# Scale columns first: the first four heads without the shift, key groups on demand, and two moved side tasks

## The chip, the cores and the metric

One core of a Trainium2 chip runs the whole program. The metric is device time in microseconds (us), from repeated executions. The profiler's span is 1.7 to 1.9 us shorter than the device time of the same execution. On one core a slower state is only recognised by its distance from the fastest run. All kernels below gave correct results.

Names: PE is TensorE's matmul, PEld its weight load, DVE VectorE, ACT ScalarE, POOL GpSimd, SPq the queue that issues DMA. The kernel divides PSUM, which holds the results of matmuls, into eight banks, 0 to 7. "Granted clock" is the share of full speed that TensorE's clock was allowed.

## The reference, cut to what matters

```python
mod = (_silu(c) @ w_mod).reshape(c.shape[0], 6, 1, -1)
sa, ca, ga, sb, cb, gb = (mod[:, 0], mod[:, 1], mod[:, 2], mod[:, 3], mod[:, 4], mod[:, 5])
h = layernorm(x) * (1 + ca) + sa                 # x: 2048 x 1024
x = x + ga * attention(h, k_cache, v_cache, wq, wo)   # 32 heads of 128, 4 key groups, last 512 keys
h = layernorm(x) * (1 + cb) + sb
x = x + gb * ((silu(h @ w_gate) * (h @ w_up)) @ w_down)
```

The scale `ca` and the shift `sa` are needed before the first query projection. The rows are handled in four chunks of 512. The query of a head is `(n * (1 + ca) + sa) @ wq = (n * (1 + ca)) @ wq + sa @ wq`, where `n` is the normalised row; the second term is the same for all rows, so it is one column per head in the transposed layout that the kernel uses. The change rests on this identity.

## The kernel before

A helper waits for what each operation reads and writes; banks are such objects too. A bank can be written again only after its reader has finished. The program emits one list of instructions for each engine, in the order of the code below.

The prologue normalises the first chunk, computes scale and shift as 128 matmuls with a single column each (from eight 512 KB pieces of `w_mod`), and fills TensorE in between with `warm` products on zeros. `x_mod` writes the modulated input, four heads are projected, all 16 key tiles are transposed:

```python
def mod_mm(w_ap, wbuf, k, cols):
    for n, (j, o) in enumerate(cols):
        mm(bank(XB, 1, 2 * o), w_ap[:, j * P:(j + 1) * P], sc_bf[:, k:k + 1], ...)   # XB = 7: one column
...
for k in range(4, DT):
    warm(3, WB)
    mod_k(k)                       # 16 single-column products
warm(5, WB)
x_mod()                            # hT = psum * gain + shift, on DVE and ACT
for sl in range(2):
    for kc in range(sl * HK, (sl + 1) * HK):
        for h in range(LEAD + 1):  # four heads
            mm(bank(QB0[h]), wq_s[0][:, kc, h * P:(h + 1) * P], hT[0][:, kc, :], ...)
for idx in range(GK):              # 16 key transposes into banks 1 and 2
    transpose(bank_bf(SCB + 1 + idx // 8)[...], k_nat[:, idx, :], ...)
```

The main loop has one step per head. It projects head `i+3`, computes scores of head `i-1` and the PV product of head `i-2`, then runs one step of a background list `bg`. `row_task` broadcasts a row over all partitions: POOL makes diagonal matrices, TensorE multiplies them into bank XB, DVE copies the bank:

```python
def row_task(dst, dbuf, src, sbuf):
    T.op(POOL, lambda: g.tensor_copy(c6[:, :], src), ...)
    diags(0)                                        # four POOL products, 128x128
    yield
    for n in range(2):
        for q in range(4):
            mm(bank(XB, P, q * P), ones_bf, diag[q], ...)
        T.op(DVE, lambda: V.tensor_copy(dst[:, n * 512:(n + 1) * 512], bank(XB)), writes=[PB[XB], dbuf])
        if n == 0:
            diags(1)
        yield
...
LOADT = {Hq + 2 + (5 * n) // 2: n for n in range(NL)}   # loads of the later gate columns
bg.append(rows)                    # first row task: runs in heads 1 to 3
for i in range(1, NA + 2):
    if i == 8:
        add_ln1(1)                 # layernorm of the next chunk joins the background list
    if i + LEAD < NA:
        if (i + LEAD) % Hq == 0:
            finish(ln1[(i + LEAD) // Hq])
        qproj(i + LEAD)            # bank QB, evicted by DVE
    if i - 5 in LOADT:             # gate column used five heads after its load
        mod_col(n); ...            # the last one appends the row task of the last gate
    scores(i - 1); pv(i - 2)
    if h2 == Hq - 1 and ch2 < NCH - 1:
        finish(rows)               # a row task still open is forced here
        oproj(ch2)
    run_bg(1)
```

The softmax here doesn't subtract the row's maximum and nothing guards it: scores larger than these inputs give would overflow.

## Time and profile before

| | before |
|---|---|
| median of three runs | 1282.97 us (1281.84 to 1283.47) |
| span of the profiled run | 1280.5 us |
| PE busy | 1271.3 us (99%) |
| first projection can start (scale copied) | 19.77 us |
| first exponential | 31.86 us |
| first reciprocal (first PV product finished) | 35.60 us |
| one head in the steady state | 3.50 us |

The page of the kernel before, its part on the engines and its chain of waits (the chain that ended last, by engine):

```profile
PE 1271.3 (99%) x7632; PEld 645.9 (50%) x7632; DVE 474.9 (37%) x873; ACT 339.7 (27%) x382; POOL 42.1 (3%) x102
PE 99%; DVE 0%; DMA 0%; POOL 0%; issue 0%; ACT 0%; SPq 0%; POOLq 0%
```

TensorE is the limit, so only what TensorE waits for, or does needlessly, can be won. The list of PE's waits in the kernel before (who waited for whom, us in total, times, longest):

```profile
PE ps L369 <- DMA c_row<-in_c_dram: 3.6, 1, 3.6
PE ps L266 <- DVE rowb L567: 1.5, 1, 1.5
PE ps L266 <- DVE arena L394: 0.5, 1, 0.5
PE ps L266 <- POOL arena L559: 0.3, 1, 0.3
PE ps L266 <- DVE arena L455: 0.3, 1, 0.3
PE ps L266 <- ACT arena L633: 0.2, 1, 0.2
```

The `rowb` and `L559` lines are one stall near 482 us, the `L394` line is one near 129 us. The first, in the timeline of the kernel before (start, duration, engine, line, operation; idle time before it and what ended it in brackets):

```profile
481.93 2.35 POOL L559 TENSOR_SCALAR arena<-arena,c 128x128 bf16<-128x128 bf16 x4 [0.66 <-PE ps L266]
482.56 0.68 DVE L567 CAST rowb<-ps 128x512 bf16<-128x512 f32 x1
483.39 0.59 PE L266 MATMUL ps<-arena 128*128 128x128 bf16 x3 [1.47 <-DVE rowb L567]
484.33 8.00 PE L266 MATMUL ps<-arena 128*128 128x128 bf16 x37 [0.35 <-POOL arena L559]
```

The row task of the last gate is forced at the end of the third chunk. TensorE can go on only when POOL has made the last diagonal, at 484.33 us. The second stall is seen in the reciprocals, which follow one another once a head:

```profile
125.51 0.18 DVE L651 RECIPROCAL rl<-ps 128x4 f32<-128x4 f32 x1 [1.08 <-PE ps L266]
129.01 0.18 DVE L651 RECIPROCAL rl<-ps 128x4 f32<-128x4 f32 x1 [1.08 <-PE ps L266]
133.46 0.18 DVE L651 RECIPROCAL rl<-ps 128x4 f32<-128x4 f32 x1 [1.08 <-PE ps L266]
```

The normal distance is 3.50 us; from 129.01 to 133.46 it is 4.45 us. The next chunk's modulated input had to be finished there. The same view where the first row task runs, early in the loop:

```profile
35.60 0.18 DVE L651 RECIPROCAL rl<-ps 128x4 f32<-128x4 f32 x1 [1.46 <-PE ps L266]
35.82 0.69 DVE L654 TENSOR_TENSOR arena<-ps,rl 128x512 bf16<-128x512 f32 x1
36.43 0.68 DVE L567 CAST arena<-ps 128x512 bf16<-128x512 f32 x1
39.32 0.18 DVE L651 RECIPROCAL rl<-ps 128x4 f32<-128x4 f32 x1 [1.08 <-PE ps L266]
```

The copy of bank XB (L567) ends 1.51 us after the reciprocal has begun. Here nobody waits for it: the next reciprocal comes 3.72 us later, and the extra 0.22 us are the row task's own four products.

### The profile page before, as it was taken

To read this page: it belongs to the slowest core of one execution; us is meant where nothing else is said; L and a number is where in the kernel's file an instruction comes from. 1 tells how busy PE (TensorE), PEld (TensorE's weight loads), DVE (VectorE), ACT (ScalarE), POOL (GpSimd) and SP (SyncE) were. 2 spreads that over 40 slices of the span, in tenths; PEclk is the share of its full clock that TensorE was granted. 3 is DMA by queue.
4 is the path that set the end of the run, shared out by engine and by line. 5 is a ranking of instruction groups with operands and counts; after the bars stand their busy time and mean duration, and the time that the engine had idled before them with its cause. 6 is when DMAs were issued, how large, how long until landed. Compare 5 with 4: busy or idle time off the path is not lost.

```text
span 1280.5 us, 17793 instructions
## 1 busy us (share of the span) xinstructions
PE 1271.3 (99%) x7632; PEld 645.9 (50%) x7632; DVE 474.9 (37%) x873; ACT 339.7 (27%) x382; POOL 42.1 (3%) x102
## 2 busy tenths in 40 slices
PE   8999999999999999999999999999999999999999
PEld 4565545555455554455554444444444444444444
DVE  3455324664247652265422331233222331221222
ACT  3555303555025550055520111011100111011100
POOL 2010000000000001000000000000000000000000
PEclk9999999999999999999999999999999999999999
DMA  8999403866018641065352974046421754035200
GB/s 287 264 238 238 101 1 71 194 141 157 1 24 191 145 120 41 1 128 112 73 150 70 283 239 132 17 144 169 132 74 39 199 149 132 17 114 165 67 9 25
DMA packets 233742, 155.31 MB, mean 121 GB/s; under 512 B 128960, under 2 KB 219968, under 8 KB 233664
## 3 DMA queue, kind: packets, MB, share of 16 engines
q1 hardware_dynamic: 175424, 95.45, 31.0%
q10 hardware_dynamic: 58240, 58.72, 14.4%
q8 instruction: 60, 0.98, 0.3%
q14 instruction: 18, 0.15, 0.0%
HBM read 119.54 MB, written 4.19 MB: 97 GB/s over the span
## 4 chain that ended last, share of the span: by engine, by line
PE 99%; DVE 0%; DMA 0%; POOL 0%; issue 0%; ACT 0%; SPq 0%; POOLq 0%
PE ps L266 99%; PE ps L270 0%; DMA c_row<-in_c_dram 0%; POOL arena L559 0%; ACT arena L633 0%; DVE arena L654 0%; DVE arena L455 0%; DVE tmp L673 0%; DVE arena L675 0%; SPq L302 0%; DVE arena L394 0%; DVE rl L651 0%; DVE mod_bf L449 0%; PE ps L369 0%; DVE gain L435 0%
## 5 line engine op out<-in xcount | busy, mean ns | idle before, releaser
L266 PE MATMUL ps<-arena 128*128 128x512 bf16 (+2 forms) x7391 | 1266.5, 334 | 2.9 <-DVE rowb L567 1.5
L266 PEld LDWEIGHTS ps<-arena 128*128 128x128 bf16 x7391 | 636.6, 98 | 622.9 <-issue 3.0
L633 ACT ACTIVATE arena<-ps 128x1024 bf16<-128x1024 f32 x256 | 262.0, 1024 | 355.2 <-PE ps L266 343.5
L848 ACT ACTIVATE arena<-ps 128x512 bf16<-128x512 f32 x112 | 66.9, 597 | 506.1 <-PE ps L266 506.1
L849 DVE TENSOR_TENSOR arena<-ps,arena 128x512 bf16<-128x512 f32 x112 | 77.4, 692 | 276.2 <-PE ps L266 276.2
L673 DVE TENSOR_TENSOR tmp<-ps,rowb 128x512 f32<-128x512 f32 (+1 forms) x65 | 44.4, 683 | 319.3 <-PE ps L266 319.3
L590 DVE CAST arena<-ps 128x512 bf16<-128x512 f32 x124 | 85.6, 691 | 60.0 <-PE ps L266 60.0
L654 DVE TENSOR_TENSOR arena<-ps,rl 128x512 bf16<-128x512 f32 x128 | 88.5, 691 | 4.7 <-DVE rl L651 0.3
L651 DVE RECIPROCAL rl<-ps 128x4 f32<-128x4 f32 x128 | 23.3, 182 | 120.4 <-PE ps L266 120.4
L378 DVE BATCH_NORM_STATS2 st<-x_res 128x6 f32<-128x512 bf16 x62 | 42.3, 683 | 3.6 <-DMA x_res<-in_A_x_dram 3.5
L383 POOL TENSOR_SCALAR rstd<-mv 128x1 f32<-128x1 f32 x31 | 6.9, 224 | 887.8 <-DVE mv L382 887.8
L544 DVE SCALAR_TENSOR_TENSOR arena<-arena 128x1024 bf16<-128x1024 bf16 x24 | 29.2, 1215 | 0.0
L675 DVE TENSOR_TENSOR arena<-tmp,x_res 128x512 bf16<-128x512 f32 (+1 forms) x33 | 22.3, 676 | 1.1
L675 DVE TENSOR_TENSOR x_res<-tmp,x_res 128x512 bf16<-128x512 f32 x32 | 22.1, 692 | 1.1
L394 DVE TENSOR_SCALAR arena<-arena,gain,mod_bf 128x512 bf16<-128x512 bf16 x56 | 20.3, 405 | 0.0
L385 POOL TENSOR_TENSOR rstd<-rstd,mhalf 128x1 f32<-128x1 f32 x31 | 17.7, 570 | 2.6
L389 DVE TENSOR_SCALAR nsc<-x_res,mv,rstd 128x1024 bf16<-128x1024 bf16 x30 | 16.1, 538 | 0.9 <-POOL rstd L385 0.9
L559 POOL TENSOR_SCALAR arena<-arena,c 128x128 bf16<-128x128 bf16 x24 | 14.5, 620 | 23.9 <-PE ps L266 23.6
L266 PEld LDWEIGHTS ps<-sc_bf,arena 128*128 128x128 bf16 x192 | 7.1, 96 | 3.8
L266 PE MATMUL ps<-sc_bf,arena 128*128 128x1 bf16 x192 | 7.1, 163 | 0.0
L382 DVE BATCH_NORM_AGGREGATE mv<-st 128x2 f32<-128x12 f32 x31 | 6.5, 208 | 1.1
L459 ACT ACTIVATE arena<-ps,mod_bf,gain_f 128x512 bf16<-128x512 bf16 x3 | 2.2, 774 | 11.1 <-DVE arena L455 11.1
(44 smaller groups left out, 33.0 us busy)
## 6 DMA issues: line engine op xcount, KB each, us to landing
arena<-in_A_wq_dram SPq DMA_DIRECT2D x31, 1024.0 KB, 5.6
arena<-in_B_w_gate_dram ACTq DMA_DIRECT2D x28, 1024.0 KB, 5.3
arena<-in_B_w_up_dram ACTq DMA_DIRECT2D x28, 1024.0 KB, 7.9
arena<-in_A_wo_dram SPq DMA_DIRECT2D x8, 1024.0 KB, 6.1
arena<-in_B_w_down_dram SPq DMA_DIRECT2D x7, 1024.0 KB, 9.3
arena<-in_w_mod_dram SPq DMA_DIRECT2D x8, 512.0 KB, 8.2
out_dram<-arena SPq DMA_DIRECT2D x15, 256.0 KB, 2.0
x_res<-in_A_x_dram SPq DMA_DIRECT2D x3, 1024.0 KB, 6.4
```

The source lines that it names most:

```text
L266: T.op(PE, lambda: TE.matmul(out_ap, lhsT, rhs, start=start, stop=stop, skip_group_check=skip), reads=reads, writes=[bank_buf])
L378: T.op(DVE, lambda: V.bn_stats(st_[sl][:, hf * 6:hf * 6 + 6], x_res[:, t, hf * 512:hf * 512 + 512]), reads=[B_x[t]], writes=[B_st[sl]])
L394: T.op(DVE, lambda: V.tensor_scalar(dst[:, dt, :], dst[:, dt, :], gain[gi][:, dt:dt + 1], mod_bf[:, ccol + dt:ccol + dt + 1], op0=ALU.mult ...
L544: T.op(DVE, lambda: V.scalar_tensor_tensor(mt[n % 2], mt[n % 2], 1.0, sc_row, op0=ALU.mult, op1=ALU.mult, accum_out=mcol[:, n:n + 1]), rea ...
L590: T.op(DVE, lambda: V.tensor_copy(qT_s[qs], bank(QB)), writes=[PB[QB], B_qT[qs]])
L633: T.op(ACT, lambda: A.activation(ex_s[es][:, 2 * kp:2 * kp + 2, :], banks2(SCB + 2 * kp), AF.Exp, scale=att_scale), writes=[PB[SCB + 2 * k ...
L651: T.op(DVE, lambda: V.reciprocal(rl[r][:, :].rearrange("p (a b) -> p a b", a=2), psap(PVB * 512 + P, [[512, 2], [130, 2]])), writes=both + ...
L654: T.op(DVE, lambda: V.tensor_tensor(o_s[os_].rearrange("p (a b) d -> p a b d", a=2), psap(PVB * 512, [[512, 2], [130, 2], [1, P]]), rlb, A ...
L673: T.op(DVE, lambda: V.tensor_tensor(tmp[s][:, 0:n], bank(b, n), rowb[ri][:, c0:c0 + n], ALU.mult), reads=[B_row[ri]], writes=[PB[b], B_tmp ...
L675: T.op(DVE, lambda: V.tensor_tensor(dst[:, c0:c0 + n], tmp[s][:, 0:n], x_res[:, t, c0:c0 + n], ALU.add), reads=[B_tmp[s], B_x[t]], writes= ...
L848: T.op(ACT, lambda: A.activation(sg_s[ss], bank(gb), AF.Silu), writes=[PB[gb], B_sg[ss]])
L849: T.op(DVE, lambda: V.tensor_tensor(guT[:, ft, :], bank(ub), sg_s[ss], ALU.mult), reads=[B_sg[ss]], writes=[PB[ub], B_gu[ft]])
```

## The change

The intent: have the first projection wait for the scale columns only (2 MB of `w_mod` instead of 4 MB), bring the shift in later as one bias column per head for the first four heads, add it to the input for all others, transpose the key groups when they are needed, and start two background tasks earlier. The diff, cut to its core:

```diff
-            wme = [... eight pieces of scale and shift columns, 512 KB each ...]
+            wca = [... eight pieces of scale columns, 256 KB each, loaded first ...]
+            wsa = [... shift columns, loaded behind the first weights of the projection ...]
@@ prologue
-                mod_k(k)                    # 16 products, with warm(2) or warm(3)
+                mod_ca(k)                   # 8 products, with warm(2) or warm(1)
-                        ... V.tensor_scalar(hT[0][:, dt, :], src, gain, mod_bf, op0=ALU.mult, op1=ALU.add)
+                        ... V.tensor_scalar(hT[0][:, dt, :], src, gain, None, op0=ALU.mult)
@@ behind the projection of the first four heads
-            for idx in range(GK): transpose(...)            # all 16 key tiles
+            for k in range(DT):
+                mod_mm(wsa[:, k, :], B_wsa[k], k, MCOLS)    # 64 single-column products: the shift
+            T.op(DVE, ... mod_bf[:, 0:DT] <- bank XB)
+            k_turn(0, SCB + 1)                              # 4 key tiles
+            for h in range(LEAD + 1):                       # 32 single-column products: the bias
+                for kc in range(DT):
+                    mm(bank(SCB + 2, 1, 2 * h), wq_s[0][:, kc, h * P:(h + 1) * P], mod_bf[:, kc:kc + 1], ...)
+            for dt in range(DT):                            # hT += shift, in place
+                if dt < 4: DVE   elif dt < 6: ACT   else: POOL
+            ... the four evictions add bq[:, h:h + 1] (DVE and ACT)
@@ main loop
-            LOADT = {Hq + 2 + (5 * n) // 2: n for n in range(NL)}
+            LOADT = {Hq + 2 + (9 * n) // 4: n for n in range(NL)}
+                if 2 <= i < 1 + Hkv:
+                    k_turn(i - 1, XB)                       # key groups 1 to 3 through bank XB
+                    T.op(DVE, lambda: V.tensor_copy(kd, ks), writes=[PB[XB], B_kT[i - 1]])
-                if i == 8:
+                if i == 5:
                     add_ln1(1)
-                    qproj(i + LEAD)
+                    qproj(i + LEAD, SCB + 3 if i == 1 else QB)
-                if i - 5 in LOADT:
+                if i - 4 in LOADT:
```

The change also merges two reciprocal square roots on POOL into one and reorders some loads.

More of the change, by code (lines that the diff above doesn't have):

```diff
@@ L193, in bass_adaLN_cond__sliding_block_cached__swiglu_ffn__prompt_kernel @@
     mv = [S_("mv%d" % i, [P, 2], F32) for i in range(4)]
-    rstd = [S_("rstd%d" % i, [P, 1], F32) for i in range(4)]
+    rstd4 = S_("rstd4", [P, 4], F32)
+    rstd = [rstd4[:, i:i + 1] for i in range(4)]
+    bq = S_("bq", [P, 4], F32)
     rl = [S_("rl%d" % i, [P, 4], F32) for i in range(2)]
@@ L232, in bass_adaLN_cond__sliding_block_cached__swiglu_ffn__prompt_kernel @@
     B_cT = _Buf("cT"); B_sc = _Buf("sc"); B_late = [_Buf("late%d" % i) for i in range(4)]; B_c6 = _Buf("c6"); B_mcol = _Buf("mcol"); B_scr = _Buf("scr")
-    B_mode = _Buf("mode"); B_gf = _Buf("gf")
+    B_mode = _Buf("mode"); B_modc = _Buf("modc"); B_bq = _Buf("bq"); B_gf = _Buf("gf")
     B_nm = _Buf("nmean"); B_acc = _Buf("acc")
@@ L321, in _ @@
             HK = DT // 2
-            B_wme = [_Buf("wme%d" % k) for k in range(DT)]
-            wme = [arena.at(OFF_OT + k * 4 * KB, [NE * P], BF16, [B_wme[k]]) for k in range(DT)]
+            B_wca = [_Buf("wca%d" % k) for k in range(DT)]
+            B_wsa = [_Buf("wsa%d" % k) for k in range(DT)]
+            wca = [arena.at(OFF_OT + k * 2 * KB, [D], BF16, [B_wca[k]]) for k in range(DT)]
+            wsa = arena.at(OFF_OT + 16 * KB, [DT, D], BF16, B_wsa)
             for k in range(DT):
-                T.op(dq("q_wm%d" % k), lambda: SP.dma_start(wme[k], w_mod[k * P:(k + 1) * P, 0:NE * P]), writes=[B_wme[k]])
+                T.op(dq("q_wca%d" % k), lambda: SP.dma_start(wca[k], w_mod[k * P:(k + 1) * P, D:2 * D]), writes=[B_wca[k]])
             NWQ = 2
@@ L347, in _ @@
             load_wq0(1)
+            for k2 in range(DT // 2):
+                T.op(dq("q_wsa%d" % k2), lambda: SP.dma_start(
+                    wsa[:, 2 * k2:2 * k2 + 2, :],
+                    w_mod[2 * k2 * P:(2 * k2 + 2) * P, 0:D].rearrange("(k p) n -> p k n", p=P)), writes=B_wsa[2 * k2:2 * k2 + 2])
             B_kn = [_Buf("kn%d" % i) for i in range(Hkv)]
-            B_kT = _Buf("kT"); B_kT2 = _Buf("kT2"); B_va = _Buf("va")
-            k_nat = arena.at(OFF_KN, [GK, P], BF16, B_kn)
-            kT_sb = arena.at(OFF_KT, [GK, P], BF16, [B_kT, B_kT2])
+            B_kT = [_Buf("kT%d" % i) for i in range(Hkv)]
+            B_va = _Buf("va")
+            kT_sb = arena.at(OFF_KT, [GK, P], BF16, B_kT)
             VW = 160
@@ L356, in _, with load_k @@
             B_vg = [_Buf("vg%d" % i) for i in range(Hkv)]
-            for gk in range(Hkv):
+            hT = [arena.at(OFF_HT + i * 8 * KB, [DT, CH], BF16, []) for i in range(2)]
+            B_hT = [[_Buf("hT%d_%d" % (i, dt)) for dt in range(DT)] for i in range(2)]
+            for i in range(2):
+                arena.regs.append((OFF_HT + i * 8 * KB, OFF_HT + (i + 1) * 8 * KB, B_hT[i]))
+            k_nat = hT[1].rearrange("p a b -> p (a b)")[:, 0:GK * P].rearrange("p (a b) -> p a b", a=GK)
+            def load_k(gk):
                 T.op(Q_k[gk], lambda: SP.dma_start(k_nat[:, gk * KT:(gk + 1) * KT, :],
@@ L360, in _, with load_v @@
                      writes=[B_kn[gk]])
-            load_wq(1)
-            for gk in range(Hkv):
+            def load_v(gk):
                 T.op(Q_v[gk], lambda: SP.dma_start(v_aug[:, gk * KT:(gk + 1) * KT, 0:P],
@@ L365, in _ @@
                      writes=[B_vg[gk]])
+            load_k(0)
+            load_wq(1)
+            load_v(0)
+            load_x(1)
+            for gk in range(1, Hkv):
+                load_k(gk)
+            for gk in range(1, Hkv):
+                load_v(gk)
             T.op(POOL, lambda: g.memset(v_aug[:, :, P:P + 2], 1.0), writes=[B_va])
@@ L382, in aggr @@
                 T.op(DVE, lambda: V.bn_aggr(mv[sl][:, :], st_[sl][:, :]), reads=[B_st[sl]], writes=[B_mv[sl]])
-                T.op(POOL, lambda: g.tensor_scalar(rstd[sl][:, :], mv[sl][:, 1:2], eps, None, op0=ALU.add),
+                T.op(POOL, lambda: g.tensor_scalar(rstd[sl], mv[sl][:, 1:2], eps, None, op0=ALU.add),
                      reads=[B_mv[sl]], writes=[B_rs[sl]])
-                T.op(POOL, lambda: g.tensor_tensor(rstd[sl][:, :], rstd[sl][:, :], mhalf[:, 0:1], ALU.pow),
+                T.op(POOL, lambda: g.tensor_tensor(rstd[sl], rstd[sl], mhalf[:, 0:1], ALU.pow),
                      reads=[B_rs[sl], B_mh], writes=[B_rs[sl]])
             def norm(t, sl, ns):
-                T.op(DVE, lambda: V.tensor_scalar(nsc4[ns], x_res[:, t, :], mv[sl][:, 0:1], rstd[sl][:, 0:1],
+                T.op(DVE, lambda: V.tensor_scalar(nsc4[ns], x_res[:, t, :], mv[sl][:, 0:1], rstd[sl],
                                                   op0=ALU.subtract, op1=ALU.mult),
@@ L416, in ln_task @@
                         yield
-            hT = [arena.at(OFF_HT + i * 8 * KB, [DT, CH], BF16, []) for i in range(2)]
-            B_hT = [[_Buf("hT%d_%d" % (i, dt)) for dt in range(DT)] for i in range(2)]
-            for i in range(2):
-                arena.regs.append((OFF_HT + i * 8 * KB, OFF_HT + (i + 1) * 8 * KB, B_hT[i]))
             def mod_mm(w_ap, wbuf, k, cols):
@@ L448, in x_mod @@
             def x_mod():
-                T.op(DVE, lambda: V.tensor_copy(mod_bf[:, 0:NE], psap(XB * 512, [[2, NE]])), writes=[PB[XB], B_mode])
-                mod_gain(0, 0, DT, B_mode, B_g[0])
+                T.op(DVE, lambda: V.tensor_copy(mod_bf[:, DT:NE], psap(XB * 512, [[2, DT]])), writes=[PB[XB], B_modc])
+                mod_gain(0, 0, DT, B_modc, B_g[0])
                 T.op(DVE, lambda: V.tensor_copy(gain_f[:, :], gain[0][:, :]), reads=[B_g[0]], writes=[B_gf])
@@ L454, in x_mod, with mod_ca @@
                     if dt % 2 == 0 or dt == 5:
-                        T.op(DVE, lambda: V.tensor_scalar(hT[0][:, dt, :], src, gain[0][:, dt:dt + 1], mod_bf[:, dt:dt + 1],
-                                                          op0=ALU.mult, op1=ALU.add),
-                             reads=[B_g[0], B_mode], writes=[PB[dt // 2], B_hT[0][dt]])
-                    else:
-                        T.op(ACT, lambda: A.activation(hT[0][:, dt, :], src, AF.Identity,
-                                                       bias=mod_bf[:, dt:dt + 1], scale=gain_f[:, dt:dt + 1]),
-                             reads=[B_gf, B_mode], writes=[PB[dt // 2], B_hT[0][dt]])
-            ECOLS = [(j, j) for j in range(NE)]
-            def mod_k(k):
-                mod_mm(wme[k], B_wme[k], k, ECOLS)
+                        T.op(DVE, lambda: V.tensor_scalar(hT[0][:, dt, :], src, gain[0][:, dt:dt + 1], None, op0=ALU.mult),
+                             reads=[B_g[0]], writes=[PB[dt // 2], B_hT[0][dt]])
+                    else:
+                        T.op(ACT, lambda: A.activation(hT[0][:, dt, :], src, AF.Copy, scale=gain_f[:, dt:dt + 1]),
+                             reads=[B_gf], writes=[PB[dt // 2], B_hT[0][dt]])
+            MCOLS = [(j, j) for j in range(DT)]
+            def mod_ca(k):
+                mod_mm(wca[k], B_wca[k], k, MCOLS)
             tl = TPC - 1
-            def rstd_pow(t):
-                T.op(POOL, lambda: g.tensor_tensor(rstd[t][:, :], rstd[t][:, :], mhalf[:, 0:1], ALU.pow),
-                     reads=[B_rs[t], B_mh], writes=[B_rs[t]])
             T.op(ACT, lambda: A.activation(nsc4[tl], x_res[:, tl, :], AF.Copy, accum_out=acc[:, 0:1]),
@@ L496, in _ @@
             for k in range(3):
-                mod_k(k)
+                mod_ca(k)
                 warm(2, WB)
             stats(2, 2, 1)
-            aggr(2)
-            T.op(POOL, lambda: g.tensor_scalar(rstd[tl][:, :], acc[:, 1:2], 1.0 / D, eps, op0=ALU.mult, op1=ALU.add),
+            T.op(DVE, lambda: V.bn_aggr(mv[2][:, :], st_[2][:, :]), reads=[B_st[2]], writes=[B_mv[2]])
+            T.op(POOL, lambda: g.tensor_scalar(rstd[2], mv[2][:, 1:2], eps, None, op0=ALU.add),
+                 reads=[B_mv[2]], writes=[B_rs[2]])
+            T.op(POOL, lambda: g.tensor_scalar(rstd[tl], acc[:, 1:2], 1.0 / D, eps, op0=ALU.mult, op1=ALU.add),
                  reads=[B_acc], writes=[B_rs[tl]])
-            rstd_pow(tl)
+            T.op(POOL, lambda: g.tensor_tensor(rstd4[:, 2:4], rstd4[:, 2:4], mhalf[:, 0:2], ALU.pow),
+                 reads=[B_mh], writes=[B_rs[2], B_rs[tl]])
             norm(2, 2, 2)
             x_first(2)
-            warm(3, WB)
-            T.op(DVE, lambda: V.tensor_scalar(nsc4[tl], x_res[:, tl, :], nmean[:, 0:1], rstd[tl][:, 0:1],
+            warm(1, WB)
+            T.op(DVE, lambda: V.tensor_scalar(nsc4[tl], x_res[:, tl, :], nmean[:, 0:1], rstd[tl],
                                               op0=ALU.add, op1=ALU.mult),
                  reads=[B_x[tl], B_nm, B_rs[tl]], writes=[B_ns4[tl]])
-            mod_k(3)
+            for k in range(3, 5):
+                mod_ca(k)
+                warm(1, WB)
             x_first(3)
-            for k in range(4, DT):
-                warm(3, WB)
-                mod_k(k)
+            for k in range(5, DT):
+                warm(1, WB)
+                mod_ca(k)
             warm(5, WB)
@@ L579, in _, with qproj @@
             Q_tr = [dq("q_tr%d" % i) for i in range(NOS)]
-            def qproj(i):
+            def qproj(i, b=QB):
                 ch, h = divmod(i, Hq)
@@ L586, in qproj @@
                 for kc in range(DT):
-                    mm(bank(QB), wq_s[sl][:, kc, hh * P:(hh + 1) * P], hT[ch % 2][:, kc, :], kc == 0, kc == DT - 1,
-                       [B_wq[sl][kc // HK], B_hT[ch % 2][kc]], PB[QB])
+                    mm(bank(b), wq_s[sl][:, kc, hh * P:(hh + 1) * P], hT[ch % 2][:, kc, :], kc == 0, kc == DT - 1,
+                       [B_wq[sl][kc // HK], B_hT[ch % 2][kc]], PB[b])
                 qs = i % NQT
-                T.op(DVE, lambda: V.tensor_copy(qT_s[qs], bank(QB)), writes=[PB[QB], B_qT[qs]])
@@ L593, in _ @@
-            QB0 = [QB, PVB, PVB + 1, SCB]
+                T.op(DVE, lambda: V.tensor_copy(qT_s[qs], bank(b)), writes=[PB[b], B_qT[qs]])
+            QB0 = [PVB, PVB + 1, SCB, QB]
             LEAD = 3
-            for sl in range(2):
-                for kc in range(sl * HK, (sl + 1) * HK):
-                    for h in range(LEAD + 1):
-                        mm(bank(QB0[h]), wq_s[0][:, kc, h * P:(h + 1) * P], hT[0][:, kc, :], kc == 0, kc == DT - 1,
-                           [B_wq[0][sl], B_hT[0][kc]], PB[QB0[h]])
@@ L600, in _ @@
-            for idx in range(GK):
-                b = SCB + 1 + idx // 8
-                transpose(bank_bf(b)[:, (idx % 8) * P:(idx % 8 + 1) * P], k_nat[:, idx, :], [B_kn[idx // KT]], PB[b])
-            def q_evac(h):
-                return (lambda: V.tensor_copy(qT_s[h], bank(QB0[h]))) if h % 2 == 0 else (
-                    lambda: A.activation(qT_s[h], bank(QB0[h]), AF.Copy))
-            def k_evac(bi):
-                dst = kT_sb[:, bi * 8:bi * 8 + 8, :]
-                src = bank_bf(SCB + 1 + bi).rearrange("p (a b) -> p a b", a=8)
-                return (lambda: V.tensor_copy(dst, src)) if bi == 0 else (lambda: A.activation(dst, src, AF.Copy))
@@ L613, in _ @@
-            T.op(DVE, q_evac(0), writes=[PB[QB0[0]], B_qT[0]])
-            T.op(ACT, q_evac(3), writes=[PB[QB0[3]], B_qT[3]])
-            T.op(DVE, k_evac(0), writes=[PB[SCB + 1], B_kT])
-            T.op(ACT, k_evac(1), writes=[PB[SCB + 2], B_kT2])
-            T.op(DVE, q_evac(2), writes=[PB[QB0[2]], B_qT[2]])
-            T.op(ACT, q_evac(1), writes=[PB[QB0[1]], B_qT[1]])
+            for kc in range(DT):
+                for h in range(LEAD + 1):
+                    mm(bank(QB0[h]), wq_s[0][:, kc, h * P:(h + 1) * P], hT[0][:, kc, :], kc == 0, kc == DT - 1,
+                       [B_wq[0][kc // HK], B_hT[0][kc]], PB[QB0[h]])
@@ new lines, in _, with k_turn, k_evac @@
+            for k in range(DT):
+                mod_mm(wsa[:, k, :], B_wsa[k], k, MCOLS)
+            def k_turn(gk, b):
+                for kt in range(KT):
+                    transpose(bank_bf(b)[:, kt * P:(kt + 1) * P], k_nat[:, gk * KT + kt, :], [B_kn[gk]], PB[b])
+            def k_evac(gk, b):
+                return (kT_sb[:, gk * KT:(gk + 1) * KT, :], bank_bf(b)[:, 0:KT * P].rearrange("p (a b) -> p a b", a=KT))
+            T.op(DVE, lambda: V.tensor_copy(mod_bf[:, 0:DT], psap(XB * 512, [[2, DT]])), writes=[PB[XB], B_mode])
@@ new lines, in _ @@
+            k_turn(0, SCB + 1)
+            kd, ks = k_evac(0, SCB + 1)
+            T.op(ACT, lambda: A.activation(kd, ks, AF.Copy), writes=[PB[SCB + 1], B_kT[0]])
+            for h in range(LEAD + 1):
+                for kc in range(DT):
+                    mm(bank(SCB + 2, 1, 2 * h), wq_s[0][:, kc, h * P:(h + 1) * P], mod_bf[:, kc:kc + 1],
+                       h == 0 and kc == 0, kc == DT - 1, [B_wq[0][kc // HK], B_mode], PB[SCB + 2], skip=True)
+            for dt in range(DT):
+                d = hT[0][:, dt, :]
+                if dt < 4:
+                    T.op(DVE, lambda: V.tensor_scalar(d, d, mod_bf[:, dt:dt + 1], None, op0=ALU.add),
+                         reads=[B_mode], writes=[B_hT[0][dt]])
+                elif dt < 6:
+                    T.op(ACT, lambda: A.activation(d, d, AF.Identity, bias=mod_bf[:, dt:dt + 1]),
+                         reads=[B_mode], writes=[B_hT[0][dt]])
+                else:
+                    T.op(POOL, lambda: g.tensor_scalar(d, d, mod_bf[:, dt:dt + 1], None, op0=ALU.add),
+                         reads=[B_mode], writes=[B_hT[0][dt]])
@@ new lines, in _ @@
+            T.op(DVE, lambda: V.tensor_copy(bq[:, :], psap((SCB + 2) * 512, [[2, LEAD + 1]])), writes=[PB[SCB + 2], B_bq])
+            for h in (0, 2, 3, 1):
+                if h < 2:
+                    T.op(DVE, lambda: V.tensor_scalar(qT_s[h], bank(QB0[h]), bq[:, h:h + 1], None, op0=ALU.add),
+                         reads=[B_bq], writes=[PB[QB0[h]], B_qT[h]])
+                else:
+                    T.op(ACT, lambda: A.activation(qT_s[h], bank(QB0[h]), AF.Identity, bias=bq[:, h:h + 1]),
+                         reads=[B_bq], writes=[PB[QB0[h]], B_qT[h]])
@@ L630, in scores @@
                 for kt in range(KT):
-                    mm(bank(SCB + kt), kT_sb[:, gk * KT + kt, :], qT_s[qs], True, True, [[B_kT, B_kT2][gk // 2], B_qT[qs]], PB[SCB + kt])
+                    mm(bank(SCB + kt), kT_sb[:, gk * KT + kt, :], qT_s[qs], True, True, [B_kT[gk], B_qT[qs]], PB[SCB + kt])
                 for kp in range(KT // 2):
@@ L710, in add_ln2 @@
                 bg.append(ln2[ch])
-            LOADX = {1: 1, 19: 2, 40: 3}
-            LOADT = {Hq + 2 + (5 * n) // 2: n for n in range(NL)}
+            LOADX = {19: 2, 40: 3}
+            LOADT = {Hq + 2 + (9 * n) // 4: n for n in range(NL)}
             LOADO = {5 + (21 * p) // 8: p for p in range(8)}
@@ L726, in _ @@
                     load_wo(LOADO[i])
-                if i == 8:
+                if 2 <= i < 1 + Hkv:
+                    k_turn(i - 1, XB)
+                    kd, ks = k_evac(i - 1, XB)
+                    T.op(DVE, lambda: V.tensor_copy(kd, ks), writes=[PB[XB], B_kT[i - 1]])
+                    if i == Hkv:
+                        for b_ in B_hT[1]:
+                            for kb in B_kn:
+                                b_.absorb(kb)
+                if i == 5:
                     add_ln1(1)
@@ L742, in _ @@
                         bg.insert(0, rows)
-                if i - 5 in LOADT:
-                    n = LOADT[i - 5]
+                if i - 4 in LOADT:
+                    n = LOADT[i - 4]
                     mod_col(n)
```

## The prediction

> **What bounds it now.** The page gives TensorE 1271.3 us busy of a 1280.5 us span; the chain of waits is 99% TensorE. The list of TensorE waits leaves little to win: 3.6 us for the first load; 0.3 us for the first modulated tile; about 1 us in the first heads, where it waits for the exponentials; one stall near 129 us and one near 482 us. In steady state one head takes 3.50 us from one reciprocal to the next (timeline of VectorE), bound by TensorE. Only the first 35 us and those two stalls can change.
>
> **The two late stalls (gain about 3.1 us).** At 129 us the interval between reciprocals is 4.45 us instead of 3.50: the next chunk's modulation runs just before its projection. Starting that chunk's layernorm at head 5 instead of 8 should remove these 0.95 us. At 482 us the row task for the last gate is forced at the chunk's end: TensorE stands from 481.9 to 484.3 us for GpSimd's four diagonal products (2.35 us) and the row copy; 2.2 us are lost. Loads every 9/4 heads end it some six heads earlier, so this goes too.
>
> **Prologue (gain about 0.4 us at the first PV product).** TensorE runs without a gap there to 20.7 us, so DMA is not what binds. 64 of the 128 single-column products and nine warm-up products (0.21 us each) leave it: the first projection should start near 17.3 us instead of 20.95. Given back behind the projection: 64 shift products (16 took 0.41 us, so 1.65 us), their copy, 32 bias columns (0.8 us), four shift additions on VectorE (0.41 us each), bias copy, evictions (0.69 us), two ScalarE evictions and the table load (1.28 us). I place the first exponential near 31.0 us instead of 31.86. The shift additions on GpSimd gate the fifth head's projection: one 128x128 product took 620 ns, a one-column operation 224 ns; scaled, an estimate of 1.8 us each for 128x512. The Trainium skill ("GPSIMD Engine Reference", section 3.1, elementwise) gives 769 ns for 512 elements at its best; the trace's 620 ns for 128 says slower. With 1.8 us this projection ends near 30.4 us, and little of the 0.8 us is left; hence 0.4.
>
> **New stalls (loss about 3.5 us).** Key groups 2 and 3 are transposed at the start of heads 3 and 4 into the bank that the row task uses. The compiled order puts them straight behind the row task's four products, waiting for VectorE. VectorE first does reciprocal, normalisation and row copy: before, the copy ended 1.51 us after the reciprocal began (35.60 to 37.11 us), and TensorE did not wait for it. Now it does, about 1.5 us, twice, plus 0.45 us for the eight transposes themselves, which lie in a TensorE-bound stretch (16 took 0.89 us before, in the prologue; the first two groups are inside the prologue's sum).
>
> **Sum.** +3.1 + 0.4 - 3.0 - 0.45 = about 0. I lean slightly to a gain: 1282.5 us, 80% range 1280.3 to 1284.6 us. Faster by over 2%: 0.005; within 2%: 0.99; slower: 0.005.
>
> **What would show each step.** First projection at 17 to 18 us; first exponential at 30.5 to 31.5 us; GpSimd's 128x512 additions at 1.3 to 2 us; TensorE waiting about 1.5 us twice for the row copy before the key transposes near 36 and 40 us; no wait near 129 and 482 us; everything after 490 us unchanged in length.
>
> **What would make it wrong.** GpSimd additions far slower or faster; scale columns landing after 15 us, so that the projection starts later; a TensorE gap long enough to lower its clock (the skill's "TensorE: Matmul & The Clock Gate", Part 1, puts that at about 3.4 us idle; no such gap is in this trace); the row task no longer adjacent to the transposes.

## The result, and the profile after

| | before | after |
|---|---|---|
| median of four runs each | 1282.77 us (1281.84 to 1283.47) | 1283.17 us (1282.82 to 1283.94) |
| ratio after / before | | 1.0004, 95% interval 0.9987 to 1.0022 |
| span of the profiled run | 1280.5 us | 1282.1 us |
| scale copied | 19.77 us | 16.42 us |
| first exponential | 31.86 us | 32.17 us |
| first reciprocal | 35.60 us | 36.90 us |

The two kernels are the same within the noise. But inside the trace, much has moved. Subtracting the times of the 128 reciprocals (one per head) and of the later activations in the two profiled runs gives this ledger; the sum is the difference of the spans up to rounding:

```
what                                             us, after minus before
up to the first reciprocal                        +1.30
next head (reciprocal to reciprocal)              +1.85    5.57 us instead of 3.72
the head after it                                 +1.85    5.57 us instead of 3.72
heads 3 to 26                                      0.00
head 27 (near 129 us before)                      -0.95    3.50 us instead of 4.45
rest of attention, to the end of the third chunk  -2.41    row task of the last gate
from there to the end                              0.00
sum                                               +1.64
```

(In the third chunk the earlier row task first adds 0.45 us of its own products, which the end of the chunk then saves: -2.86 there, -2.41 in all.) The part of the page on the engines, after:

```profile
PE 1264.0 (99%) x7513; PEld 646.4 (50%) x7655; DVE 477.4 (37%) x881; ACT 340.2 (27%) x384; POOL 44.5 (3%) x103
```

This line does not help. PE records are missing here (7513 against 7655 weight loads), so its lower busy time is no gain, and 99% hides all that follows. The list of PE's waits after answers the one shown of before:

```profile
PE ps L393 <- DMA c_row<-in_c_dram: 3.7, 1, 3.7
PE ps L272 <- DVE arena L584: 2.9, 2, 1.5
PE ps L268 <- DVE mod_bf L627: 0.6, 1, 0.6
PE ps L268 <- DVE bq L646: 0.2, 1, 0.2
```

The two late stalls are gone. New is a wait for DVE's copy of the row task (L584), twice. Its place, in the timeline after:

```profile
36.90 0.18 DVE L686 RECIPROCAL rl<-ps 128x4 f32<-128x4 f32 x1 [1.08 <-PE ps L268]
37.12 0.69 DVE L689 TENSOR_TENSOR arena<-ps,rl 128x512 bf16<-128x512 f32 x1
37.73 0.68 DVE L584 CAST arena<-ps 128x512 bf16<-128x512 f32 x1
38.55 0.38 PE L272 MATMUL ps<-arena 128*128 128x128 bf16 x4 [1.47 <-DVE arena L584]
42.47 0.18 DVE L686 RECIPROCAL rl<-ps 128x4 f32<-128x4 f32 x1 [1.08 <-PE ps L268]
44.13 0.38 PE L272 MATMUL ps<-arena 128*128 128x128 bf16 x4 [1.47 <-DVE arena L584]
```

The key transposes (L272) go into bank XB, which the row task has just filled; they wait until DVE has done the reciprocal, the normalisation and the copy. In the trace PE runs nothing else in these 1.47 us. The reciprocals after, in the place of the former stall near 129 us:

```profile
127.02 0.18 DVE L686 RECIPROCAL rl<-ps 128x4 f32<-128x4 f32 x1 [1.08 <-PE ps L268]
130.51 0.18 DVE L686 RECIPROCAL rl<-ps 128x4 f32<-128x4 f32 x1 [1.08 <-PE ps L268]
134.01 0.18 DVE L686 RECIPROCAL rl<-ps 128x4 f32<-128x4 f32 x1 [1.08 <-PE ps L268]
```

All steps are 3.50 us. Last, the prologue: the busy time in windows (window, its length, then the busy time and the number of instructions of PE, PEld, DVE, ACT, POOL; then the granted clock, the DMA share and GB/s). First the kernel before, then the one after:

```profile
30.00:32.00 2.00, 2.00 (x11) 0.75 (x10) 0.69 (x1) 1.97 (x4) 0.00 (x0) 1.00 0.99 329
32.00:34.00 2.00, 1.84 (x9) 0.64 (x7) 0.55 (x1) 1.91 (x3) 0.00 (x0) 1.00 1.07 355
```

```profile
24.00:28.00 4.00, 3.38 (x102) 2.85 (x101) 0.93 (x3) 0.83 (x2) 0.70 (x1) 1.00 1.08 360
28.00:30.00 2.00, 1.61 (x14) 0.65 (x12) 1.97 (x6) 1.70 (x4) 2.00 (x2) 0.94 0.90 177
30.00:32.00 2.00, 1.99 (x6) 0.48 (x4) 1.37 (x3) 1.83 (x2) 1.91 (x4) 0.50 0.96 301
32.00:34.00 2.00, 2.00 (x11) 1.06 (x10) 0.44 (x2) 1.73 (x2) 1.22 (x3) 0.70 1.07 362
```

The column before the DMA share is the surprise: the granted clock is 0.50 from 30 to 32 us. The trace's clock record puts it at 29.77 to 33.18 us, 3.41 us long. "PE 1.99 of 2.00 busy" in that window means six matmuls, where eleven ran before. The completion times of the matmuls, which the trace has as semaphore events, show both what came before this and what it did:

```
after: completion of PE's instructions (us), and the distance between them
24.39 - 24.82   512 columns, real data     216 ns each
24.86 - 27.01   64 single columns (shift)   34 ns each    2.19 us
27.04 - 27.15   4 key transposes            34 ns each
27.45 - 28.54   32 single columns (bias)    34 ns each    (0.30 us of waiting before the first)
28.75 - 29.65   three of 512 columns        210, 260, 639 ns (waiting for the shift additions)
30.25 - 33.01   512 columns                 383, 426, 625, 425, 426, 426, 426 ns   (one of 216 ns at 29.86 left out)
from 33.38      512 columns                 216 ns again
```

For 4.4 us, from 24.8 to 29.2, TensorE was given little but products of one column. The completions on PE never lay further apart than 0.64 us, and yet the clock fell. One thing has to be kept apart here. The *starts* of the 64 shift products lie 25 ns apart in the trace, and the first key transpose starts 1.60 us after the first of them; it is the completion signals that lie 34 ns apart, those of the four transposes behind them too (elsewhere 56 ns). So the signals lag behind, and who waits for the last one waits 2.19 us. In the profile page this stretch looks nearly busy.

### The profile page after: what moved, and what is told of

It reads as the page before. It is cut to its first block, busy times and chain, and to the rows that moved or that the text cites. A ratio compares the mean times of both kernels' runs of the same rounds, so it can differ in the third digit from the quotient of the medians.

```text
span 1282.1 us, 17720 instructions
## 1 busy us (share of the span) xinstructions
PE 1264.0 (99%) x7513; PEld 646.4 (50%) x7655; DVE 477.4 (37%) x881; ACT 340.2 (27%) x384; POOL 44.5 (3%) x103
## 4 chain that ended last, share of the span: by engine, by line
PE 98%; issue 1%; DVE 1%; DMA 0%; SPq 0%
PE ps L268 98%; PE ps L272 0%; DMA c_row<-in_c_dram 0%; DVE arena L638 0%; DVE arena L689 0%; DVE arena L584 0%; DVE rl L686 0%; DVE tmp L708 0%; DVE arena L710 0%; SPq L304 0%; DVE arena L474 0%; PE ps L393 0%; DVE gain L454 0%; DVE mod_bf L468 0%; DVE gain_f L470 0%
## 5 line engine op out<-in xcount | busy, mean ns | idle before, releaser
L268 PE MATMUL ps<-arena 128*128 128x512 bf16 (+1 forms) x7240 | 1257.3, 333 | 8.0 <-DVE bq L646 0.2
L561 DVE SCALAR_TENSOR_TENSOR arena<-arena 128x1024 bf16<-128x1024 bf16 x24 | 29.2, 1215 | 0.0
L272 PE MATMUL ps<-arena 128*128 128x128 bf16 x32 | 2.9, 228 | 2.9 <-DVE arena L584 2.9
```

The source lines that it names most:

```text
L268: T.op(PE, lambda: TE.matmul(out_ap, lhsT, rhs, start=start, stop=stop, skip_group_check=skip), reads=reads, writes=[bank_buf])
L561: T.op(DVE, lambda: V.scalar_tensor_tensor(mt[n % 2], mt[n % 2], 1.0, sc_row, op0=ALU.mult, op1=ALU.mult, accum_out=mcol[:, n:n + 1]), rea ...
```

## The experiments

Two questions. First, do the new stalls and the two moved tasks account for the loop? Second, why did the prologue cost 1.30 us where the prediction had a gain of 0.4? For the prologue there are two theories. *Clock*: the stretch of single-column products makes the clock fall, and what follows runs at half speed. *Gate*: the shift additions (POOL's above all) and the evictions behind them set the time, and the clock falls in a wait. To be free of differences in the start, prologues are compared from the copy of the scale (the first CAST on DVE) to the first reciprocal: 15.83 us before, 20.48 us after.

The changed kernel was not run again in the rounds of the experiments. Differences to its median (1283.17 us) are across batches, in which the kernel before had medians of 1282.77, 1283.14 and 1282.89 us, so they hold to some 0.4 us; before_narrow, before_wide, dve_adds and lean ran on another chip than the other four. A mean clock below 1.000 says that the clock fell somewhere in a run; where, only a profile shows. All outputs are right.

### rows_late: the first row task behind the next chunk's layernorm

```diff
-            bg.append(rows)
             for i in range(1, NA + 2):
@@
                 if i == 5:
                     add_ln1(1)
+                    bg.append(rows)
```

> The changed kernel, with the first row task queued behind the next chunk's layernorm, so that key groups 2 and 3 are no longer transposed straight behind it. Theory: the two head intervals of 5.57 us lose the 1.6 us of waiting each and end near 3.72 us (0.22 us of transposes stay), so the whole is about 3.2 us shorter than the changed kernel (about 1280.0 us). Rival: the bank conflict only hides another limit (exponentials or the fifth head's projection), and less than 1 us comes back.

Measured: 1279.91 us median (1279.42 to 1280.5, five runs), ratio to before 0.9978 (0.9965 to 0.9990). That is 3.26 us below the median of the changed kernel. The timeline of this kernel, its first reciprocals:

```profile
36.10 0.18 DVE L686 RECIPROCAL rl<-ps 128x4 f32<-128x4 f32 x1 [1.08 <-PE ps L268]
39.83 0.18 DVE L686 RECIPROCAL rl<-ps 128x4 f32<-128x4 f32 x1 [1.08 <-PE ps L268]
43.55 0.18 DVE L686 RECIPROCAL rl<-ps 128x4 f32<-128x4 f32 x1 [1.08 <-PE ps L268]
```

The intervals are 3.73 and 3.72 us, as expected: the stalls were the bank conflict and nothing else. The transposes themselves stay, at 0.22 us a head; the row task's own products now come in two later heads, 27 and 28, and cost 0.22 us there each. The row's data is needed only from head 38 on, so the delay costs nothing.

The same run tells something of the prologue, by luck. Its instructions on PE up to the first PV product are those of the changed kernel, but in its profiled execution the clock stayed at 1.00:

```profile
30.00:32.00 2.00, 1.47 (x7) 0.41 (x6) 1.49 (x3) 1.97 (x4) 0.72 (x1) 1.00 0.98 281
```

From the scale's copy to the first reciprocal it took 19.58 us instead of 20.48. So the low clock was worth 0.90 us in the profile after. (POOL's diagonals come later here too; interleave and combo below differ in the same way and both take 18.32 us, so they do not matter. The medians are too noisy to show the 0.90 us.) By their mean clocks (0.998 or 0.999 instead of 1.000), four of the five timed runs of this kernel and three of the four of the changed kernel had a fall.

### before_late: the kernel before, with the two moved tasks only

```diff
-            LOADT = {Hq + 2 + (5 * n) // 2: n for n in range(NL)}
+            LOADT = {Hq + 2 + (9 * n) // 4: n for n in range(NL)}
-                if i == 8:
+                if i == 5:
-                if i - 5 in LOADT:
-                    n = LOADT[i - 5]
+                if i - 4 in LOADT:
+                    n = LOADT[i - 4]
```

> The kernel before, with only the two schedule edits of the change: next chunk's layernorm at head 5 instead of 8, gate-column loads every 9/4 heads used four heads later. Theory: the waits near 129 us (0.95 us) and 482 us (2.4 us) vanish and nothing else moves: about 3.4 us faster than before (1279.5 us). Rival: they return elsewhere, for instance as waits for the transposing loads, and less than 1.5 us is gained.

Measured: 1278.87 us median (1278.23 to 1281.0, five runs), ratio 0.9971 (0.9959 to 0.9984); the kernel before had 1283.14 us in these rounds, so the medians differ by 4.3 us, more than expected. In its trace 0.96 us went at head 27 and 2.41 us by the end of the third chunk, 3.37 us together, as expected. The list of PE's waits for this kernel:

```profile
PE ps L369 <- DMA c_row<-in_c_dram: 3.5, 1, 3.5
PE ps L266 <- DMA arena<-in_w_mod_dram: 0.4, 1, 0.4
PE ps L266 <- DVE arena L455: 0.3, 1, 0.3
PE ps L266 <- ACT arena L633: 0.2, 1, 0.2
```

Neither stall is left. This part of the change is good on its own. And rows_late, which has the new prologue as well, is 1.0 us slower than before_late by the medians, so the rest of the change gains nothing even without the stalls. In the two profiles, both at full clock there, it is 0.66 us: 0.44 us are the key transposes that now lie in the loop, and 0.22 us come before the first reciprocal, no more than the 0.29 us by which before and before_late differ there.

### interleave: the shift products among the projections

```diff
             for kc in range(DT):
                 for h in range(LEAD + 1):
                     mm(bank(QB0[h]), wq_s[0][:, kc, h * P:(h + 1) * P], hT[0][:, kc, :], ...)
-            for k in range(DT):
-                mod_mm(wsa[:, k, :], B_wsa[k], k, MCOLS)
+                if HK - 1 <= kc < DT - 1:
+                    for k in (2 * (kc - HK + 1), 2 * (kc - HK + 1) + 1):
+                        mod_mm(wsa[:, k, :], B_wsa[k], k, MCOLS)
@@ behind the 32 bias products
+            warm(3, SCB + 3)
```

> The changed kernel, with the 64 shift products set between the first four heads' projections (behind the input tiles 3 to 6) and three warm-up products behind the bias columns. Theory clock: the stretch of single-column products from 24.8 to 28.5 us made the granted clock fall to 0.5 from 29.8 to 33.2 us; broken up, the clock stays 1.0, the fifth head's projection and the first scores run at 216 ns instead of 426, and the first reciprocal comes 1.5 to 2.0 us earlier (36.9 to about 35.2 us). Rival gate: the shift additions on GpSimd (end 30.6 us) and the eviction behind them set the time, the low clock only fills a wait; the reciprocal moves by under 0.5 us.

Measured: 1281.3 us median (1280.9 to 1281.79, five runs), ratio 0.9988 (0.9976 to 1.0001), 1.87 us below the changed kernel; all five runs have a mean clock of 1.000 (the profile of this run has no clock record, but its 512-column products behind the bias products complete 216 ns apart). The first reciprocal came at 34.73 us, 2.17 us earlier, and the stretch from the scale's copy took 18.32 us instead of 20.48. Against the 19.58 us without a fall of the clock, 1.26 us come from something else: with the products earlier, the shift's copy is ready before the projection ends, and the shift additions start 9.52 us after the scale's copy (in the combined kernel, same code) instead of 10.81. That is 1.29 us. So both theories hold a part: 0.90 us clock, about 1.3 us that the additions came late behind 64 products and their copy. Two things about this run: the three warm-up products came with the same edit, and what they do for the clock by themselves was not tested. And the 16 single-column products in each gap put off the next large product by only 0.40 us, 25 ns each, as the starts say: the lag of their signals is made up while the large products run.

### combo: both edits

> Both edits at once. If stalls and clock are the causes and independent, the two gains add: about 5 us faster than the changed kernel, near 1278.2 us, which beats the kernel before by over 4 us. If they share a wait, less than the sum.

Measured: 1277.65 us median (1277.64 to 1278.4, five runs), ratio 0.9961 (0.9948 to 0.9975). The gains (3.26 and 1.87 us) add to 5.13; measured are 5.52 us against the changed kernel. All five runs have a clock of 1.000. The list of PE's waits has one line left:

```profile
PE ps L393 <- DMA c_row<-in_c_dram: 3.6, 1, 3.6
```

### before_narrow and before_wide: the clock by itself

To separate the products from the waits around them, both kernels put useless products on real operands behind the four projections of the kernel before, into the unused bank 3:

```diff
+            for n in range(224):                 # before_wide: range(36), and 512 columns for 1
+                mm(bank(SCB + 3, 1, 0), wq_s[0][:, n % DT, 0:P], hT[0][:, n % DT, 0:1], True, True, ...)
```

> The kernel before with 224 single-column products on real data set behind the first four heads' projections, writing to an unused bank (result unchanged). By the 34 ns at which such products complete in the trace of the changed kernel they take 7.65 us. Theory (they do not count as work for the granted clock): the clock falls to 0.5 for one or two stretches of 3.4 us around 30 to 40 us, and the first reciprocal moves by 7.65 us plus 1 to 2 us. Rival (the fall came from the waits around them, not from the products): the clock stays 1.0 and it moves by 7.6 us.

> Control for the run of 224 single-column products: 36 products of 512 columns in the same place, by 216 ns each 7.8 us. Both theories: the clock stays at 1.0 and the first reciprocal moves by 7.8 us, no more.

Windows of before_narrow, then of before_wide (columns as above; the granted clock stands third from the end):

```profile
32.00:34.00 2.00, 2.00 (x64) 2.00 (x62) 0.00 (x0) 0.00 (x0) 0.00 (x0) 0.90 0.03 8
34.00:37.00 3.00, 3.00 (x55) 3.00 (x54) 0.50 (x1) 0.00 (x0) 0.00 (x0) 0.50 0.03 5
37.00:40.00 3.00, 2.78 (x8) 1.03 (x7) 0.79 (x2) 2.79 (x3) 0.00 (x0) 0.50 0.80 241
```

```profile
32.00:34.00 2.00, 2.00 (x11) 0.91 (x10) 0.00 (x0) 0.00 (x0) 0.00 (x0) 1.00 0.00 0
34.00:37.00 3.00, 2.95 (x26) 1.84 (x26) 0.87 (x2) 0.43 (x1) 0.00 (x0) 1.00 0.04 9
37.00:40.00 3.00, 3.00 (x15) 1.26 (x14) 1.11 (x2) 2.97 (x4) 0.00 (x0) 1.00 0.99 300
```

In the narrow run the completions follow without a gap (34 ns each, as measured before), PE and even PEld are fully busy, and the clock falls all the same, from 33.59 to 40.42 us. In the control it stays at 1.00 there. From the scale's copy to the first reciprocal the narrow one took 24.75 us and the wide one 23.60; the base is 15.83, so the added time is 8.92 and 7.77 us, where the products alone are about 7.65 and 7.8. The low clock cost about 1.3 us, or about 2.1 us if the products are counted by their starts: the first transpose starts 6.81 us after the first of them, the first 96 at steps of 25 ns and the others at 34. All four narrow runs have a mean clock of 0.996 or 0.997, the wide ones 1.000, 0.999, 0.999 and 0.997; so it is the profiles that separate the two, one of each. Here it is the single-column products that do it, not the waits. (Medians: 1292.57 and 1291.38 us. Later parts of the narrow trace also drift from the control, 1.7 us more by the end, which we have not explained; only the prologue is used.)

The control shows one thing more. After the stall at the end of the third chunk, which here lies near 489 us, its profile has this:

```profile
489.00:492.00 3.00, 1.10 (x13) 0.65 (x12) 1.47 (x3) 1.02 (x1) 2.34 (x4) 1.00 0.85 240
492.00:497.00 5.00, 4.95 (x16) 1.89 (x16) 0.69 (x1) 0.00 (x0) 0.00 (x0) 0.66 0.35 92
```

With PE busy for 1.10 of 3.00 us the clock fell behind the stall (492.88 to 496.30 us by the record), and that part of the program took 1.68 us more than in the profiled run of the kernel before. The narrow trace has the same: a fall from 494.39 to 497.81 us behind this stall, and 1.61 us more. Among the 18 runs of the kernel before in the two batches, five have a mean clock of 0.999; they average 1283.66 us, the other thirteen 1282.58. It is likely, though shown by two profiles only, that the 2.4 us stall sometimes costs more than its length, and that before_late gained more than its trace for this reason.

### dve_adds: the combined kernel without additions on POOL

```diff
                 else:
-                    T.op(POOL, lambda: g.tensor_scalar(d, d, mod_bf[:, dt:dt + 1], None, op0=ALU.add), ...)
+                    T.op(DVE, lambda: V.tensor_scalar(d, d, mod_bf[:, dt:dt + 1], None, op0=ALU.add), ...)
```

> The combined kernel with the two shift additions of GpSimd moved to VectorE. Theory (in the combined kernel TensorE waits for no addition, and VectorE's evictions start the exponentials): the evictions start 0.8 us later, so the first exponential is later and the whole 0.3 to 0.9 us slower. Rival (GpSimd's 1.66 us additions are the gate of the prologue): 0.5 us or more faster.

Measured: 1277.94 us median (1277.66 to 1279.27, five runs), ratio 0.9964 (0.9951 to 0.9978). From the scale's copy to the first reciprocal it took 18.32 us, to the hundredth what the combined kernel took. Both expectations missed. The additions show why. First the combined kernel (minimum, median, maximum in ns), POOL's and DVE's, then dve_adds, DVE's first four:

```profile
L646 POOL TENSOR_SCALAR arena<-arena,mod_bf x2: 1591/1664/1737, 25.1 to 26.8; 128x512 bf16<-128x512 bf16 x2
L640 DVE TENSOR_SCALAR arena<-arena,mod_bf x4: 341/536/783, 25.0 to 26.3; 128x512 bf16<-128x512 bf16 x4
```

```profile
L640 DVE TENSOR_SCALAR arena<-arena,mod_bf x4: 348/348/354, 25.1 to 25.9; 128x512 bf16<-128x512 bf16 x4
```

With POOL working beside it, DVE's same additions take up to 783 ns; alone, 348 ns. So DVE does six additions in 1.67 us, where it had done four in 1.95. Moving two additions to POOL won nothing. The Trainium skill says it in "GPSIMD Engine Reference", section 8, Key points: GpSimd shares its SBUF interfaces with VectorE and contends with some of its instructions. This trace agrees: 348 against 341 to 783 ns.

### lean: the combined kernel with eight fewer warm-up products

```diff
             for k in range(3):
                 mod_ca(k)
-                warm(2, WB)
+                warm(1, WB)
@@ behind the third normalised tile, and in both later loops
-                warm(1, WB)
```

(The edits take out nine products: three in the first loop, one behind the third tile, two and three in the later loops. The note says eight; nine times 0.216 us would be 1.9 us.)

> The combined kernel with eight of the warm-up products between the scale columns taken out. Theory: TensorE alone bounds the stretch up to the first projection, so eight times 0.216 us, about 1.7 us, are gained (near 1276 us), unless the sparser stretch makes the clock fall. Rival: loads or normalisations bound it by then and less than 0.7 us is gained; or the clock falls to 0.5 and it gets slower.

Measured: 1276.96 us median (1276.57 to 1277.15, five runs), ratio 0.9953 (0.9940 to 0.9965), all at a clock of 1.000. In the traces it is 1.07 us ahead of the combined kernel at the first reciprocal and stays there; the medians differ by 0.7 us. The scale's copy comes at 14.47 instead of 15.53 us. The expectation of 1.7 us was too high. A likely part of it, not tested: the profiled run of the combined kernel reached its full clock earlier (6.82 us against 8.97). This is the fastest version: it beats the kernel before by 0.5% (5.9 us between the medians of the same rounds; the combined kernel had 5.5 in its own) and the changed kernel by 6.2 us of medians.

## Why the prediction was right or wrong

The sum was right: 1282.5 predicted, 1283.17 measured, inside the range of 1280.3 to 1284.6. Part of that is luck. One term, the prologue, was wrong by 1.7 us; the medians differ by only 0.4 us where the ledger has 1.64: the profiled run of the kernel before (1282.29 us) lay below its median and that of the changed kernel (1283.94 us) was the slowest of its four. With the ledger's 1.64 us the sum would have been 1284.4, just inside the range. Point by point:

- **The two late stalls: right.** Predicted 3.1 us of gain, 0.95 and 2.2; in the trace 0.95 and 2.41. before_late shows the same by itself, 3.37 us.
- **The new stalls: right in place, cause and size.** "About 1.5 us, twice, plus 0.45 us"; the profile has two waits of 1.47 us for the row copy, and 2 x 1.85 = 3.70 us in the intervals (a stall of 1.63 and transposes of 0.22 each), against 3.45 predicted. rows_late takes the stalls away without removing any work, which shows the cause.
- **The prologue: wrong, by 1.7 us.** Predicted a gain of 0.4 us at the first PV product, measured a loss of 1.30. The first exponential came at 32.17 us, outside the 30.5 to 31.5 given. The start was nearly as said: the projection's first weights were loaded at 17.50 us (17.3 predicted). Two terms failed. First, "64 shift products (16 took 0.41 us, so 1.65 us)": 0.41 us was counted by the *starts* in the profile. TensorE did get through the 64 in 1.60 us by their starts, but the shift's copy waits for the last completion signal, and these come 34 ns apart: 2.19 us. So the copy began at 27.03 us, TensorE stood 0.62 us for it, and the first addition began at 27.23. Second, the granted clock. "A TensorE gap long enough to lower its clock" was listed under what would make it wrong, and set aside since there is no such gap. The clock fell without a gap, and cost 0.90 us (20.48 against 19.58 us for the same instructions on PE). With the start, 0.2 us later than predicted, these are about the 1.7 us.
- **POOL's additions: right**, 1.59 to 1.74 us against an estimate of 1.8. The figure that the Trainium skill gives as the best case in "GPSIMD Engine Reference", section 3.1 (769 ns for 512 elements), was indeed not reached. But their cost to DVE, 341 to 783 ns instead of 348, was left out.
- **After 490 us: right.** The difference stays at 1.64 us from the first reciprocal of the last chunk to the end.

What made the forecast good was not the prologue, where the change's intent lay, but reading the compiled order of one bank, and the moved background tasks. The change has a gain of 3.4 us, a loss of 3.7 us, and a prologue that lost 1.3 us in the profiled run instead of winning. That is why a large rewrite moved the time so little.

What stays open: how much work a stretch needs for the clock to stay up (the changed kernel had a fall in three of four timed runs; with its products among the projections there was none in the 20 runs of interleave, combo, dve_adds and lean), and why one run of before_late (1281.0 us, mean clock 0.999) also had a fall.

The clock records give a hint of why a fall comes in one run and not in the next. They change on a grid: from the start of the full clock to the first fall it is 20.48 us in the changed kernel, 23.89 in before_narrow and 484.69 in before_wide, which is 6, 7 and 142 times 3.413 us. In before_narrow the two steps of the grid just before and in the fall's first half (30.18 to 37.01 us) are, by the completions, filled with single-column products but for the last 0.8 us. In the two profiles in which the clock fell behind the stall of the third chunk, the stall (from the last completion before it to 512-column products again) lies wholly or for the most part within one step; in the kernel before, which had no fall, a step ended at 483.34 us, within the stall of 481.94 to 484.57. And of the step in question three 512-column products were completed in the changed kernel (26.36 to 29.77 us), four in rows_late (26.65 to 30.06). So whether the clock falls seems to depend on how little TensorE does within one step, and where the steps lie differs from run to run. This is read from five traces and was not tested.

## What to carry to other kernels

When work is moved into an in-order loop, list for each bank or buffer it borrows who used it just before in program order; a conflict of two short tasks costs the whole reply time of the engine that empties the bank (here 1.5 us for 0.2 us of work), and moving one of the tasks was free. Do not move small matmuls together into one block: set them between large ones, so that nobody waits for the whole block and the clock has a better chance to stay up. Count what they take from TensorE by the starts, but what a waiter pays by the completions. And split a change that does several things: here the plain half alone (before_late) was worth more than the whole.

## What the Trainium skill lacked or had wrong

- "TensorE: Matmul & The Clock Gate", in "Why this matters for your kernels", advises "No PE-idle gaps >~3µs between matmul bursts": gaps are not the only cause. 224 single-column products in a row, 34 ns apart and without any gap, brought the clock to 0.5 for 6.83 us; 36 products of 512 columns in the same place left it at 1.0. The window of 3413 ns in the page's Part 1 agrees: the falls here lasted 3.41 us, or twice that.
- The same page, Part 2, "Back-to-back issue gap": it gives about 131 ns per matmul for 512 columns and about 81 ns for 128 as sustained values in a stream of weight loads and matmuls. Here, with a weight load for every matmul, completions lie 216 ns apart for 512 columns and 56 ns for transposes of 128 columns; those are the figures that the same section gives for the isolated gap. For a single column the page has an issue floor of about 25 ns; the starts here agree (25 ns), while completions are 34 ns apart.
- "GPSIMD Engine Reference", section 8, names the contention with VectorE and gives no size there ("SBUF — State Buffer", "Who interferes with whom", treats it at more length): 128x512 bf16 additions took 348 ns on VectorE alone and 341 to 783 ns beside GpSimd.
- No page has this for single-column products in a row: 64 of them start 25 ns apart (1.60 us up to the next instruction), but their completions are signalled 34 ns apart, so the last comes after 2.19 us. The nearest is the TensorE page's Part 3, "The cost: per-tile semaphore tail", which has completion increments of packed tiles serialize.
